# A new order, annealed offline, for the matmuls, evictions and elementwise steps of an attention and snake-MLP kernel

## The chip, the cores and the metric

The kernel runs on one core of one Trainium2 chip. The metric is the device time of an execution in microseconds (us). A core has five engines that each run their own list of instructions in order: TensorE (PE: matmuls and transposes), VectorE (DVE), ScalarE (ACT), GpSimd (POOL), and SyncE (SP), which here only issues DMAs. They wait for each other through semaphores. DMAs are issued by SP, POOL and ACT and run on sixteen DMA engines. Matmul results land in PSUM, which has eight banks of 128 partitions x 512 f32.

## The reference

Inputs are `x` [8, 8, 512, 64] (batch, head, token, dim), `state` [8, 8, 32, 64], `w_in` [512, 2048], `w_out` [2048, 512], `alpha` [2048]; all f32.

```python
scores = scale * x @ state.T; a = softmax(scores);   xread = a @ state      # [8, 8, 512, 64]
scores2 = scale * state @ x.T; a2 = softmax(scores2); sread = a2 @ x         # [8, 8, 32, 64]
y = concatenate([xread, sread], axis=2), heads moved into columns            # [8 * 544, 512]
h = y @ w_in
g = h + sin(alpha * h)**2 / (alpha + 1e-9)
out = g @ w_out                                                              # [4352, 512] f32
```

## The kernel before

All matmuls are bf16 with f32 accumulation. The 4352 rows are worked in nine tiles: tiles t = 0 to 7 hold the 512 `xread` rows of a batch, tile 8 the 256 `sread` rows of all batches. `xread @ w_in` is never built in two steps: for each batch b the kernel makes M = state @ w_in (step `m`, 64x512 pieces on quarters of the array, L488), evacuates it (`me`, L496), and then h = A @ M, where A is the normalised softmax.

The program is a list of steps in a string, `ORDER`. Each word is a method of `Steps` and its arguments; running the list in order appends instructions to the engines' lists, and nothing reorders them later (`tc.manual_schedule()`). So the list fixes the order on each engine; in time, an instruction starts when its engine is free and its semaphores are there. The last letter of many steps picks the engine: A is ACT, V is DVE, G is POOL. The steps that matter here:

- `li.s`, `lo.s`, `lx.b`: loads of a quarter of `w_in` (L282), of `w_out` (L294), of a batch of `x` (L275), all issued by POOL with a cast to bf16.
- `warm_up.n.cols.bank` (L303): n matmuls on zeros, whose result nobody reads.
- `pk.b`, `td.b`: `x` repacked on DVE and transposed by a DMA issued by SP (L389); `sc`, `ex`, `rs`, `rr`, `nm`: scores on PE, exp on ACT, row sums, reciprocal, and the multiply (L201) that makes A; `ad.b`: A transposed by a DMA from SP (L440). Batches 0 and 1 use PE transposes for some of this (`xtq`, `xt`, `at`, copied by `xc`, `ac`).
- `w`, `cs`, `rc`, `xs`: the `sread` side; eight times, once for each batch, feeding tile 8.
- `h.t.f.bank` (L537; L543 for tile 8): the 128-column piece f (0 to 15) of h for tile t, two matmuls of 512 columns (four of 256 for tile 8), into a PSUM bank. `hg` (L552) does one of the two.
- `si.t.f` (L560): sin on ACT, reading the bank. `sq.t.f.E` (L201 on DVE or POOL, L569 on ACT): its square. `gt.t.f` (L576): on DVE, gT = square / alpha + h, reading the bank again. Only after `gt` is the bank free.
- `o.t.st.f0.f1[.bank]` (L587): for row block st (four in a tile, two in tile 8), matmuls of gT piece f by `w_out`, f from f0 to f1, accumulating sixteen in one bank. `oc.t.st.E` (L595) evacuates the bank to an o_sb buffer, `os.t.st` stores it from SP (L602, for tile 8 L605). The last block, 7.3, is cut in columns into 384 and 128 (`oh`, `och`, `osh`).

A PSUM bank holds one thing at a time: a step that names a bank waits for the last reader of what was there. The s and squared-s tiles share ten buffers, gT has 38, o_sb has six.

Of the kernel before, what the change touches and what calls it, by code (L numbers as in the profile page):

```python
# [33 lines left out]
me.1.1.1.A warm_up.2.128.2 gt.0.2 si.0.0 warm_up.2.128.2 warm_up.2.128.6 warm_up.2.128.3
warm_up.2.128.2 warm_up.2.128.6 me.0.1.0.A gt.0.1 sq.0.0.G m.0.2.3.2 si.0.3 m.1.2.5.6 hg.0.4.0.7
me.0.2.0.V me.0.2.1.A hg.0.4.1 sq.0.3.G hg.0.6.0.4 me.1.2.1.V hg.0.6.1 si.0.4 hg.0.7.0.3 hg.0.11.0.2
me.1.2.0.V si.0.6 hg.0.7.1 sq.0.4.G hg.0.5.0.6 gt.0.0 hg.0.5.1 si.0.7 hg.0.11.1 hg.0.8.0.5 hg.0.8.1
sq.0.6.A gt.0.3 sq.0.7.G o.0.3.0.2.0 si.0.5 gt.0.4 o.0.3.2.3 o.0.0.0.2.1 si.0.11 o.0.0.2.3 gt.0.6
sq.0.5.G o.0.0.3.4 o.0.2.0.1.7 si.0.8 o.0.3.3.5 sq.0.11.A gt.0.7 hg.0.9.0.4 sq.0.8.G o.0.2.1.2
gt.0.5 o.0.2.2.4 hg.0.9.1 gt.0.11 o.0.0.4.5 hg.0.10.0.3 si.0.9 o.0.2.4.5 gt.0.8 o.0.0.5.6 o.0.3.5.6  # L40
sq.0.9.A o.0.3.6.8 pk.1.0.V hg.0.10.1 xt.1.1.6 pk.1.1.V si.0.10 gt.0.9 xt.1.0.2 xc.1.1.0.A sq.0.10.G
o.0.2.5.6 xc.1.1.1.V xc.1.0.0.A o.0.0.6.7 xc.1.0.1.V o.0.0.7.8 o.0.2.6.7 sc.1.1.5 gt.0.10 sc.1.0.4
m.0.3.6.2 ex.1.0 o.0.2.7.8 me.0.3.0.V o.0.1.0.3.3 me.0.3.1.V o.0.1.3.6 hg.0.13.0.6 o.0.1.6.7 ex.1.1
rs.1.0 hg.0.13.1 m.1.3.2.4 si.0.13 o.0.1.7.8 rr.1.0 rs.1.1 nm.1.0.0.4.G o.0.1.8.9 hg.0.12.0.5
o.0.3.8.9 rr.1.1 hg.0.12.1 me.1.3.0.V o.0.0.8.9 nm.1.1.0.4.G o.0.1.9.10 o.0.0.9.10 me.1.3.1.V
si.0.12 o.0.0.10.11 o.0.3.9.11 sq.0.13.G ad.1 hg.0.15.0.2 sq.0.12.A o.0.1.10.12 hg.0.15.1 gt.0.12
o.0.2.8.10 si.0.15 o.0.2.10.11 gt.0.13 o.0.0.11.12 hg.0.14.0.4 sq.0.15.A hg.0.14.1 o.0.3.11.13
si.0.14 gt.0.15 o.0.0.12.13 o.0.1.12.13 o.0.3.13.14 sq.0.14.A pk.2.0.V o.0.1.13.14 pk.2.1.V h.1.2.5
gt.0.14 h.1.4.6 td.2 si.1.2 lx.3.0.1 h.1.0.2 si.1.4 o.0.0.13.15 sq.1.2.V h.1.1.4 si.1.0 gt.1.2
sq.1.4.G o.0.3.14.16 si.1.1 o.0.2.11.13 sq.1.0.A oc.0.3.V h.1.6.5 sq.1.1.G gt.1.4 o.0.2.13.14 os.0.3  # L50
h.1.3.0 si.1.6 gt.1.0 o.0.1.14.16 si.1.3 sq.1.6.G h.1.13.6 gt.1.1 oc.0.1.A o.0.2.14.15 o.0.0.15.16
si.1.13 h.1.15.2 sq.1.3.G lx.4.0.1 gt.1.6 os.0.1 o.0.2.15.16 oc.0.0.A h.1.5.4 sq.1.13.V oc.0.2.V
si.1.15 h.1.7.3 os.0.0 gt.1.3 o.1.1.0.1.5 si.1.5 os.0.2 h.1.8.1 sq.1.15.G gt.1.13 o.1.1.1.2 si.1.7
o.1.2.0.2.7 sq.1.5.A o.1.1.2.3 sq.1.7.G h.1.12.0 gt.1.15 si.1.8 h.1.9.6 gt.1.5 o.1.2.2.3 si.1.12
sq.1.8.G o.1.2.3.5 gt.1.7 si.1.9 o.1.1.3.4 h.1.10.2 sq.1.12.A pk.3.1.V h.1.11.4 sq.1.9.G gt.1.8
o.1.2.5.6 si.1.10 o.1.2.6.7 gt.1.12 h.1.14.3 si.1.11 sq.1.10.G o.1.2.7.8 gt.1.9 sc.2.1.1 si.1.14
o.1.1.4.7 sq.1.11.A pk.3.0.V sq.1.14.G o.1.1.7.8 gt.1.10 td.3 o.1.2.8.9 sc.2.0.0 o.1.1.8.9 gt.1.11
# [24 lines left out]
o.2.2.14.15 h.3.4.4 si.3.10 gt.3.15 o.2.1.6.7 sq.3.7.G o.2.1.7.8 si.3.4 o.2.2.15.16 o.2.1.8.10
sq.3.10.A gt.3.9 o.2.1.10.11 sq.3.4.G gt.3.7 o.2.1.11.13 oc.2.2.A o.2.1.13.14 gt.3.10 o.2.1.14.16
os.2.2 h.3.3.0 gt.3.4 oc.2.1.A h.3.12.2 si.3.3 pk.5.1.V o.3.2.0.1.7 os.2.1 m.4.2.1.3.5.6 pk.5.0.V
si.3.12 sq.3.3.V td.5 o.3.3.0.1.4 me.4.2.1.V me.4.2.0.A o.3.2.1.2 sq.3.12.G o.3.3.1.2 me.4.3.0.A
o.3.2.2.3 gt.3.3 o.3.3.2.3 h.3.11.1 me.4.3.1.A gt.3.12 h.4.10.3 si.3.11 h.4.9.5 si.4.10 h.4.12.0
sq.3.11.V h.4.11.6 si.4.9 gt.3.11 sq.4.10.G o.3.2.3.5 si.4.12 o.3.2.5.7 sq.4.9.A o.3.2.7.8 gt.4.10
sq.4.12.G o.3.2.8.10 si.4.11 o.3.2.10.11 gt.4.9 o.3.3.3.5 sq.4.11.A o.3.3.5.6 gt.4.12 o.3.3.6.8
m.4.0.2.1.3.5 gt.4.11 o.3.3.8.9 me.4.1.1.V me.4.0.1.A h.3.13.0 me.4.0.0.A h.4.8.6 me.4.1.0.V
h.4.15.1 si.3.13 h.4.2.5 si.4.8 sq.3.13.V h.4.1.2 lx.6.0.1 si.4.2 gt.3.13 o.3.2.11.12 o.3.1.0.2.3  # L90
si.4.15 o.3.1.2.3 sq.4.8.V o.3.1.3.4 sq.4.2.G si.4.1 gt.4.8 o.3.3.9.12 sq.4.15.A h.4.3.0 sq.4.1.G
gt.4.2 o.3.3.12.13 h.4.13.6 si.4.3 gt.4.15 o.3.3.13.15 si.4.13 sq.4.3.G o.3.3.15.16 gt.4.1 h.4.6.5
# [65 lines left out]
class Steps:  # L158
# [449 lines left out]
    def oh(k, t, st, half, bank):  # L608
        k.o(t, st, 0, k.FT, bank, half=half)
# [54 lines left out]
```

## Time and profile before

| what | us |
|---|---|
| median of 3 runs | 221.41 (221.36 to 221.83) |
| the profiled execution's own time | 221.22 |
| its span | 219.2 |
| PE busy in the span | 211.4 |
| DVE, ACT, POOL busy | 162.9, 173.4, 106.2 |
| landings of `w_in` quarters 0, 1, 2 | 11.83, 14.91, 17.37 |

A span is the time from the first to the last instruction of the program; the time of a run also holds what lies around it. In the groups of the profile, a line reads: source line, engine, operation, output<-inputs, shape, count | busy time, mean ns of one | idle time of that engine just ahead of them and what ended it. In a table by stage, each stretch has its length, then busy time and count of PE, weight loads (PEld), DVE, ACT, POOL, then the granted PE clock, the share of the DMA engines in use, and GB/s. A PE that the profile calls busy may hold overlapping matmuls, so counts and start times are better guides than busy time.

### The profile page before, as it was taken

The page shows a single profiled execution, that of the slowest core. Times are in us where ns is not written, and L with a number is a line of the kernel's source. Part 1 is how long each engine was busy: PE and PEld are TensorE (multiplying, and loading weights), DVE is VectorE, ACT ScalarE, POOL GpSimd, SP SyncE. Part 2 cuts the span into 40 slices and gives each one's busy share as a digit, 9 for nine tenths or more (in the row PEclk, how much of TensorE's full clock was granted, in tenths as well). Part 3 has the DMA queues.
Part 4 walks back from the last instruction along what each step waited for, and adds up shares of the span by engine and source line. Part 5 has one row for each costly group of instructions (what it writes and reads, how often), then busy time and mean ns, then how long its engine had stood idle before and what let it go on. Part 6 is the DMA issues. An engine that isn't in the chain of part 4 may idle for free.

```text
span 219.2 us, 4303 instructions
## 1 busy us (share of the span) xinstructions
PE 211.4 (96%) x1593; PEld 104.5 (48%) x1619; DVE 162.9 (74%) x287; ACT 173.4 (79%) x297; POOL 106.2 (48%) x114
## 2 busy tenths in 40 slices
PE   7989999999999999999999999999999999999994
PEld 3744544444444534444454444454445555665452
DVE  3769996999787789989888788888667987661201
ACT  4799778997998979898996999798848896785111
POOL 5959533895195647753943387273501082121000
PEclk9999999999999999999999999999999999999999
DMA  6999999987491029167145327470220211012042
GB/s 195 178 206 204 205 204 146 217 169 133 101 238 48 3 92 143 57 144 96 48 79 131 109 71 96 134 110 0 48 100 0 98 48 48 0 51 96 1 143 96
DMA packets 38052, 23.48 MB, mean 107 GB/s; under 512 B 20992, under 2 KB 33680, under 8 KB 38032
## 3 DMA queue, kind: packets, MB, share of 16 engines
q1 hardware_dynamic: 26128, 15.08, 26.5%
q0 software_dynamic: 11648, 8.13, 26.0%
q8 instruction: 12, 0.20, 0.3%
q14 instruction: 8, 0.07, 0.1%
q10 hardware_dynamic: 256, 0.01, 0.1%
HBM read 17.44 MB, written 8.91 MB: 120 GB/s over the span
## 4 chain that ended last, share of the span: by engine, by line
PE 90%; DMA 6%; POOL 1%; issue 1%; ACT 0%
PE o_ps L587 54%; PE h_ps L537 22%; DMA w_in_sb<-in_moe_w_in_dram 5%; PE m_ps L488 4%; PE h_ps L543 3%; PE h_ps L552 2%; PE w_ps L450 2%; PE s_ps L399 2%; PE w_ps L461 1%; DMA s<-in_state_dram 1%; POOL w_in_sb L282 1%; PE x_ps L376 0%; POOL st_nat L267 0%; POOL s01b L255 0%; ACT o_sb L595 0%
## 5 line engine op out<-in xcount | busy, mean ns | idle before, releaser
L587 PE MATMUL o_ps<-w_out_sb,gT 128*128 128x512 bf16 (+2 forms) x542 | 133.9, 373 | 1.6 <-issue 1.0
L576 DVE SCALAR_TENSOR_TENSOR gT<-s,inva_sb,h_ps 128x512 bf16<-128x512 bf16 (+1 forms) x144 | 96.8, 713 | 20.4 <-POOL s L201 10.8
L201 POOL TENSOR_TENSOR s<-s 128x512 bf16<-128x512 bf16 (+1 forms) x75 | 75.9, 1022 | 64.4 <-ACT s L560 62.7
L560 ACT ACTIVATE s<-h_ps,alpha_sb 128x512 bf16<-128x512 f32 (+1 forms) x144 | 88.8, 670 | 11.1 <-PE h_ps L543 4.5
L587 PEld LDWEIGHTS <-gT 128*128 128x128 bf16 x560 | 52.3, 98 | 60.3 <-issue 5.0
L537 PE MATMUL h_ps<-AT,M 128*128 128x512 bf16 x219 | 60.0, 379 | 0.3
L537 PEld LDWEIGHTS <-M 128*128 128x128 bf16 x224 | 21.7, 98 | 25.9 <-issue 0.4
L569 ACT ACTIVATE s<-s 128x512 bf16<-128x512 bf16 (+1 forms) x53 | 31.4, 594 | 0.8
L201 POOL TENSOR_TENSOR A<-E,rR 128x512 bf16<-128x512 bf16 x16 | 16.6, 1056 | 23.8 <-ACT o_sb L595 12.9
L595 ACT COPY o_sb<-o_ps 128x512 f32<-128x512 f32 (+2 forms) x24 | 13.7, 570 | 16.6 <-PE o_ps L587 16.5
L496 ACT CAST M<-m_ps 128x512 bf16<-128x512 f32 x35 | 18.6, 594 | 8.2 <-PE m_ps L488 8.2
L496 DVE CAST M<-m_ps 128x512 bf16<-128x512 f32 x29 | 18.9, 679 | 2.5 <-PE m_ps L488 2.1
L595 DVE COPY o_sb<-o_ps 128x512 f32<-128x512 f32 x11 | 7.5, 685 | 12.9 <-PE o_ps L587 12.9
L201 DVE TENSOR_TENSOR s<-s 128x512 bf16<-128x512 bf16 (+1 forms) x16 | 7.0, 439 | 6.2 <-ACT s L560 6.1
L410 DVE TENSOR_REDUCE R<-E 128x16 f32<-128x512 bf16 x16 | 10.4, 657 | 0.7 <-ACT E L406 0.6
L488 PE MATMUL m_ps<-w_in_sb,stT 64*32 64x512 bf16 x256 | 10.2, 382 | 0.1
L468 DVE RECIPROCAL rC<-w_ps 128x128 f32<-128x128 f32 x8 | 7.6, 948 | 3.3 <-PE w_ps L461 3.2
L303 PE MATMUL warm_ps<-warm 128*128 128x128 bf16 (+3 forms) x66 | 8.6, 271 | 1.4 <-DVE warm L209 1.2
L552 PE MATMUL h_ps<-AT,M 128*128 128x512 bf16 x29 | 8.4, 379 | 0.9 <-ACT M L496 0.7
L406 ACT ACTIVATE E<-s_ps 128x512 bf16<-128x512 f32 x16 | 8.8, 602 | 0.4 <-PE s_ps L399 0.4
L543 PE MATMUL h_ps<-xs_all,w_in_sb 128*128 128x256 bf16 x64 | 9.1, 273 | 0.0
L543 PEld LDWEIGHTS <-w_in_sb 128*128 128x128 bf16 x64 | 6.3, 98 | 3.4
(56 smaller groups left out, 101.8 us busy)
## 6 DMA issues: line engine op xcount, KB each, us to landing
out_dram<-o_sb SPq DMA_DIRECT2D x33, 256.0 KB, 2.3
xnat<-in_x_dram POOLq DMA_DIRECT2D x7, 512.0 KB, 7.5
w_in_sb<-in_moe_w_in_dram POOLq DMA_DIRECT2D x4, 512.0 KB, 10.9
w_out_sb<-in_moe_w_out_dram POOLq DMA_DIRECT2D x4, 512.0 KB, 18.0
x<-in_x_dram SPq DMA_DIRECT2D x4, 256.0 KB, 4.2
st_nat<-in_state_dram POOLq DMA_DIRECT2D x1, 256.0 KB, 5.3
out_dram<-o_sb SPq DMA_DIRECT2D x1, 192.0 KB, 1.9
s<-in_state_dram SPq DMA_DIRECT2D x1, 128.0 KB, 2.2
```

Source lines behind the costliest of these rows:

```text
L201: {"V": k.nc.vector, "G": k.nc.gpsimd}[eng].tensor_tensor(out, a, b, ALU.mult)
L410: k.nc.vector.reduce_sum(R[:, g], k.t["E", b][:, g].rearrange("p c (h j) -> p (c h) j", j=k.Ns), axis=AX.X)
L488: k.nc.tensor.matmul(k.t["m", b, s + n, g][o0:o0 + k.Ns, :], k.stT[k.half(r), b * k.G + g, c0:c0 + k.Ns], k.w_in_sb[k.half(r), 2 * g + h, ...
L496: k.copy(eng)(k.t["M", b][:, g, s * k.FW:(s + 1) * k.FW], k.t["m", b, s, g][:])
L537: k.nc.tensor.matmul(hp[:, :n], k.t["M", t][:, g, fs], k.t["AT", t][:, g, :], start=(g == 0), stop=(g == k.G - 1),)
L543: k.nc.tensor.matmul(hp[:, :n], k.w_in_sb[:, q, fs], k.xs_all[:, q].rearrange("p b j -> p (b j)"), start=(q == 0), stop=(q == k.Q - 1),)
L552: k.nc.tensor.matmul(k.t["h", t, f][:], k.t["M", t][:, g, f * k.P:(f + 1) * k.P], k.t["AT", t][:, g, :], start=(g == 0), stop=(g == k.G - 1),)
L560: k.nc.scalar.activation(s[:, :n], k.t["h", t, f][:, :n], ACT.Sin, scale=k.alpha_sb[:, f:f + 1])
L569: k.nc.scalar.activation(s2[:, :n], s[:, :n], ACT.Square)
L576: k.nc.vector.scalar_tensor_tensor(gT[:, :n], k.t["s2", t, f][:, :n], k.inva_sb[:, f:f + 1], k.t["h", t, f][:, :n], ALU.mult, ALU.add,)
L587: k.nc.tensor.matmul(k.t["o", t, st, half][:, cols], k.t["gT", t, f][:, rows], k.w_out_sb[:, f, cols], start=(f == 0), stop=(f == k.FT - 1),)
L595: k.copy(eng)(o_sb[:, cols], k.t["o", t, st, half][:, cols])
```

## The change

The string `ORDER` is replaced as a whole. Three method changes let the new order be finer: opening a bank is a step of its own (`ho`, `oo`), `hg` and `o` issue one matmul, and the first and last matmul of an accumulation are those that come first and last in the list, so that the pieces f of an o block can be added in any order. The computation is the same; there are the same 560 o, 256 + 64 h and 256 m matmuls and the same loads, transposes and stores. Counts that differ: warm-up matmuls 66 to 14; squares on ACT 53 to 32, on DVE 16 to 55, on POOL 75 to 57; five of the sixteen `nm` move from POOL to DVE; the four casts of `x` for batch 0 (`xq`) move from ACT to DVE; M evacuations on ACT 35 to 39, on DVE 29 to 25; o evacuations on DVE 11 to 9. POOL issues its loads in the same order, SP its transposes too, with the stores at other places between them. On SP the last stores were os.6.0, 7.1, 8.1, 8.0, 7.0, 7.3 (384 columns), 7.2, 7.3 (128 columns) and become os.7.3 (384 columns), 6.3, 7.2, 7.1, 7.0, 8.1, 8.0, 7.3 (128 columns).

```diff
 ORDER = """
...
-ac.0.0.V m.0.0.6.4 m.1.0.1.2 lo.3 at.0.1.7 me.0.0.0.V me.0.0.1.A warm_up.2.128.0 warm_up.2.128.3
-me.1.0.1.A ac.0.1.V hg.0.2.0.5 me.1.0.0.V hg.0.1.0.4 hg.0.2.1 hg.0.1.1 hg.0.0.0.0 lx.2.0.1 si.0.2
-hg.0.0.1 m.1.1.6.3 si.0.1 m.0.1.7.2 hg.0.3.0.1 me.0.1.1.A sq.0.2.V hg.0.3.1 sq.0.1.G me.1.1.0.V
-me.1.1.1.A warm_up.2.128.2 gt.0.2 si.0.0 warm_up.2.128.2 warm_up.2.128.6 warm_up.2.128.3
-warm_up.2.128.2 warm_up.2.128.6 me.0.1.0.A gt.0.1 sq.0.0.G m.0.2.3.2 si.0.3 m.1.2.5.6 hg.0.4.0.7
-me.0.2.0.V me.0.2.1.A hg.0.4.1 sq.0.3.G hg.0.6.0.4 me.1.2.1.V hg.0.6.1 si.0.4 hg.0.7.0.3 hg.0.11.0.2
...
-o.8.1.1.2 oc.7.1.A o.8.1.2.3 o.8.0.0.1.6 o.8.1.3.4 os.7.1 o.8.1.4.5 h.8.14.3 o.8.1.5.7 si.8.14
-o.8.0.1.3 sq.8.14.A o.8.0.3.5 gt.8.14 o.8.0.5.7 o.8.1.7.11 o.8.0.7.15 o.8.1.11.16 o.8.0.15.16
-o.7.0.8.9 oc.8.1.A o.7.0.9.10 oc.8.0.V o.7.0.10.12 os.8.1 o.7.0.12.13 os.8.0 o.7.0.13.16 o.7.2.0.2.2
-oc.7.0.A o.7.2.2.5 os.7.0 o.7.2.5.11 oh.7.3.0.1 o.7.2.11.13 och.7.3.0.A o.7.2.13.15 osh.7.3.0
-o.7.2.15.16 oh.7.3.1.4 oc.7.2.V os.7.2 och.7.3.1.A osh.7.3.1
...
+me.0.0.1.A ac.0.1.V m.1.0.3.1 me.1.0.1.A me.1.0.0.V hg.0.0.0 li.2 hg.0.0.1 si.0.0 st_c.0.1.V
+sq.0.0.V ho.0.3.7 hg.0.3.1 lo.0 hg.0.2.0 hg.0.2.1 si.0.2 ho.0.1.3 hg.0.1.1 lo.1 m.0.1.1.6 me.0.1.0.A
+lx.1.0.1 me.0.1.1.V hg.0.1.0 si.0.1 m.1.1.0.5 me.1.1.0.A hg.0.3.0 ho.0.5.1 li.3 hg.0.5.0 hg.0.5.1
+ho.0.4.6 hg.0.4.0 lo.2 lo.3 lx.2.0.1 me.1.1.1.V ho.0.7.5 hg.0.4.1 hg.0.7.1 hg.0.7.0 gt.0.0 si.0.3
+sq.0.2.G gt.0.2 m.0.2.2.0 me.0.2.1.A sq.0.1.G gt.0.1 sq.0.3.G gt.0.3 me.0.2.0.A m.1.2.4.0 me.1.2.1.A
+ho.0.9.3 hg.0.9.1 hg.0.9.0 ho.0.11.2 hg.0.11.0 me.1.2.0.V si.0.4 sq.0.4.V gt.0.4 hg.0.11.1 ho.0.6.0
+hg.0.6.0 oo.0.1.7 si.0.5 sq.0.5.G si.0.7 sq.0.7.V hg.0.6.1 si.0.6 o.0.1.3 o.0.1.1 gt.0.7 si.0.9
+sq.0.9.V oo.0.0.4 o.0.0.1 o.0.0.3 o.0.0.0 o.0.0.2 o.0.1.0 oo.0.2.6 o.0.2.2 sq.0.6.A o.0.2.0 o.0.1.2
+o.0.2.3 gt.0.6 o.0.2.1 gt.0.9 o.0.2.4 oo.0.3.5 o.0.3.3 o.0.3.4 o.0.1.7 o.0.0.4 gt.0.5 ho.0.8.0
...
+o.0.2.5 ex.1.0 rs.1.0 sc.1.1.3 o.0.3.1 me.0.3.1.A ex.1.1 o.0.3.0 rs.1.1 ho.0.12.2 hg.0.12.0 rr.1.0
+pk.1.0.V hg.0.12.1 si.0.12 m.1.3.0.1 me.1.3.0.V me.1.3.1.A ho.0.14.3 hg.0.14.1 hg.0.14.0 o.0.0.8
...
+sq.0.15.V o.0.1.13 gt.0.15 o.0.3.13 o.0.1.15 o.0.2.15 o.0.3.15 h.1.4.1 si.1.4 h.1.6.0 si.1.6
+sq.1.6.G pk.2.0.V o.0.1.9 pk.2.1.V h.1.3.3 si.1.3 oc.0.2.V sq.1.4.V gt.1.4 sq.1.3.V gt.1.3 o.0.1.10
+h.1.7.6 si.1.7 o.0.0.13 sq.1.7.G o.0.3.11 oc.0.3.A gt.1.6 gt.1.7 h.1.13.2 si.1.13 o.0.0.15 h.1.9.1
+si.1.9 h.1.12.5 si.1.12 h.1.15.3 sq.1.9.V gt.1.9 oc.0.1.A oo.1.3.0 o.1.3.3 o.1.3.4 o.1.3.6 oc.0.0.A
+h.1.0.6 si.1.0 sq.1.13.G o.1.3.7 h.1.5.7 oo.1.2.4 o.1.2.9 o.1.2.3 o.1.2.4 o.1.2.6 gt.1.13 si.1.5
...
+osh.7.3.0 o.8.1.5 os.6.3 o.8.0.3 o.7.2.8 oc.7.2.A os.7.2 gt.8.14 o.8.1.14 o.8.0.14 o.7.0.6 o.8.1.13
+o.7.1.14 o.8.1.9 o.8.0.9 o.8.1.12 oc.7.1.A os.7.1 o.8.1.0 o.8.1.8 o.8.1.2 o.7.0.2 oc.7.0.V o.8.0.0
+os.7.0 oc.8.1.A os.8.1 o.8.0.13 o.8.0.11 oc.8.0.V os.8.0 oh.7.3.1.6 och.7.3.1.A osh.7.3.1
 """.split()
...
-        k.t = {}
+        k.t, k.made = {}, {}
...
-    def hg(k, t, f, g, *bank):
-        if g == 0:
-            k.t["h", t, f] = k.ps(bank[0], [k.P, k.S], FP32, "h_ps")
+    def ho(k, t, f, bank):
+        k.t["h", t, f] = k.ps(bank, [k.P, k.S], FP32, "h_ps")
+        k.made["h", t, f] = 0
+
+    def hg(k, t, f, g):
+        k.made["h", t, f] += 1
         k.nc.tensor.matmul(
             k.t["h", t, f][:], k.t["M", t][:, g, f * k.P:(f + 1) * k.P], k.t["AT", t][:, g, :],
-            start=(g == 0), stop=(g == k.G - 1),
+            start=k.made["h", t, f] == 1, stop=k.made["h", t, f] == k.G,
         )
...
-    def o(k, t, st, f0, f1, *bank, half=None):
+    def oo(k, t, st, bank, half=None):
+        k.t["o", t, st, half] = k.ps(bank, [k.P, k.DOUT], FP32, "o_ps")
+        k.made["o", t, st, half] = 0
+
+    def o(k, t, st, f, half=None):
         cols = k.cols(half)
-        if f0 == 0:
-            k.t["o", t, st, half] = k.ps(bank[0], [k.P, k.DOUT], FP32, "o_ps")
         rows = slice(st * k.P, (st + 1) * k.P) if t < k.B else slice(st, k.B * k.Ns, 2)
-        for f in range(f0, f1):
-            k.nc.tensor.matmul(
-                k.t["o", t, st, half][:, cols], k.t["gT", t, f][:, rows],
-                k.w_out_sb[:, f, cols], start=(f == 0), stop=(f == k.FT - 1),
-            )
+        k.made["o", t, st, half] += 1
+        k.nc.tensor.matmul(
+            k.t["o", t, st, half][:, cols], k.t["gT", t, f][:, rows], k.w_out_sb[:, f, cols],
+            start=k.made["o", t, st, half] == 1, stop=k.made["o", t, st, half] == k.FT,
+        )
...
     def oh(k, t, st, half, bank):
-        k.o(t, st, 0, k.FT, bank, half=half)
+        k.oo(t, st, bank, half=half)
+        for f in range(k.FT):
+            k.o(t, st, f, half=half)
```

## The prediction

> **What bounds the kernel now.** I read the page's totals first, then stages, then the timeline at both ends.
>
> ```profile
> span 219.2 us, 4303 instructions
> PE 211.4 (96%) x1593; PEld 104.5 (48%) x1619; DVE 162.9 (74%) x287; ACT 173.4 (79%) x297; POOL 106.2 (48%) x114
> ```
>
> TensorE is busy for 96% of the span. The stage table (busy time of each engine per stretch) says where the rest is.
>
> ```profile
> 0.00:11.85 11.85, 10.19 (x127) 6.63 (x127) 5.98 (x18) 7.45 (x14) 9.52 (x18) 1.00 0.89 187
> 11.85:17.40 5.55, 4.52 (x60) 2.13 (x60) 3.88 (x8) 5.32 (x10) 3.07 (x5) 1.00 1.24 207
> 18.20:28.00 9.80, 9.64 (x83) 4.97 (x84) 9.20 (x17) 8.67 (x16) 6.46 (x7) 1.00 1.30 204
> 28.00:208.00 180.00, 178.31 (x1260) 86.12 (x1282) 142.18 (x245) 149.88 (x256) 86.36 (x86) 1.00 0.45 92
> 216.15:219.20 3.05, 0.00 (x0) 0.00 (x0) 0.00 (x0) 0.27 (x1) 0.00 (x0) 1.00 0.31 107
> ```
>
> See the second column: after 18.2 us PE never idles for long. A dense 512-column matmul takes 0.216 us (ten in 2.16 in the chain of waits). The remaining idle is a slot of 0.216 here and there where a matmul record is missing: every record from 18.2 to 216 starts one issue time after its predecessor. So PE's end is the start of m.0.2 plus the PE work left there. Priced from dense stretches (h or o 0.216, m 0.216, sc 0.233, w 0.466, changes of tile shape 0.09 to 0.13 each way), that work is 198.6; 17.41+198.6=216.0, and the last evacuation does start at 216.15.
>
> ```profile
> 17.41 0.14 PEld L488 LDWEIGHTS <-stT 64*32 64x32 bf16 x16 [0.26 <-DMA w_in_sb<-in_moe_w_in_dram]
> 18.20 2.54 PE L552 MATMUL h_ps<-AT,M 128*128 128x512 bf16 x11 [0.16 <-issue]
> ...
> 207.87 1.49 SPq L605 DMA_DIRECT2D out_dram<-o_sb  x2
> ...
> 216.15 0.27 ACT L595 COPY o_sb<-o_ps 128x128 f32<-128x128 f32 x1 [1.50 <-PE o_ps L587]
> ```
>
> m.0.2 waits for the third w_in load (landed 17.37), which no reordering of compute brings forward. The two stores at L605 are those of tile 8, and they matter below. The profiled execution took 221.22 (span 219.2 plus 2.02 outside), 0.19 under the median; my sum is made against 221.22.
>
> **The change part by part.**
>
> *Loads, transposes, table loads: nothing.* Their order is kept on every queue, apart from stores moved between them on SP; ACT still loads its table as often. Loads run back to back, one landing per 2.54 us, so issuing lo.3 before nm instead of after lands nothing sooner. Every transpose has 3.4 us or more of PE work between its place and its use (3.2 before), except td.7, which stands beside sc.7.0 but may issue some 9 us earlier, when pk.7 is done. If that cover went, the price is a landing, 3 to 5 us. Stores free o_sb 4 us or more ahead of need.
>
> *PE work: -1.3.* Ahead of m.0.2 the new order has 14 hg matmuls where the old had 8: 6 x 0.216 = 1.30. From m.0.2 on there is one more block of m (+0.22) and one block of cs fewer (-0.2). Left at m.0.2: 197.3 instead of 198.6. The 52 dropped warm-up matmuls stood in waits for loads and are worth nothing by themselves.
>
> *New waits in the head: +2.0.* Other durations by form: si 0.695 (three in a row 1.90, so 0.633 in a queue), gt 0.742 (0.68 queued), sq 0.64 on ACT, 0.449 on DVE, 1.05 on POOL, me 0.594/0.679 (ACT/DVE); 0.2 from a matmul's issue end to its reader. (a) m.0.2 needs bank 2 (h.0.0) from gt.0.0, which on DVE stands behind st_c.0.1, sq.0.0 and both me of s=1; DVE then ends gt.0.0 at about 17.5: +0.15. (b) m.1.2 puts its second half into bank 0, which m.0.2 has just filled, and must wait for me.0.2.1 on ACT: 17.56+0.34+0.15+0.55 gives 18.66, where 17.87 is dense: +0.8. (c) Behind it on ACT stand me.0.2.0, me.1.2.1, si 4, 5, 7, 6, 9 and sq.0.6.A: 2x0.55+5x0.633+0.6 ends at 23.55; with sq.0.9.V, gt.0.6 on DVE this frees bank 0 for hg.0.8.0 at 24.37 instead of 23.97: +0.4. (d) me.1.3.0 waits on DVE behind rs, rs, rr, pk (0.66+0.66+0.25+0.43), then gt.0.12 behind it: +0.65. What is queued behind each is PE itself, in order; nothing overtakes. The old order had its evacuations of s=2 in four banks, and none of these waits shows.
>
> *New waits later: +2.3.* The old order gives the median gT 8.2 us between its chain's end and its first o; the new one 5.3, with more h and o tiles open in the eight banks. I summed queued work between a matmul's result and the PE step that needs the buffer. Early in batch 1: from si.1.4, seven si and two oc on ACT (7x0.64+2x0.58+0.2=5.9) must end before h.1.5, 5.4 us of PE work later, and a third oc before o.1.2.9: +0.7; then h.1.1 behind gt.1.14: +0.3. The same sums overrun by 0.2 to 0.5 at batch 2 (ten DVE items from sq.2.4), at batch 4's end and where batches 5 and 6 mix (fifteen DVE items from me.6.3.1). Bounds: 0.8 if only the single-queue overruns count, 4.6 if those that cross engines (s has ten buffers, and si.6.11 now waits on sq.6.4) double my hand sum. On the old order the same sums overrun nowhere (closest 0.09 to spare), as its trace shows. DVE takes 39 more sq, five nm and the x copies (163 to about 180 busy of 219): no bound by itself. nm and the x copy on DVE aren't in the trace: between 0.425 (copy) and 1.056 (nm on POOL); I take 0.45, nearest to the bf16 multiply on DVE; hidden before the w_in landing at 11.83, where the next work waits.
>
> *The tail: +2.8.* In the old order tile 8's stores issue at 207.87 and 208.76, almost eight microseconds before the last. They cost more than others: issue 0.775 and 0.609 against 0.33, and the trace's completion writes end at 211.71 and 212.89: 3.8 and 4.1 after issue, where a 256 KB store of another tile lands in 2.0. Their completions come from 8 engines each instead of 16, and the DMA rate starts low:
>
> ```profile
> 209.00:209.50 0.50, 0.50 (x4) 0.26 (x3) 0.00 (x0) 0.29 (x1) 0.00 (x0) 1.00 0.39 66
> 209.50:210.00 0.50, 0.50 (x4) 0.23 (x3) 0.00 (x0) 0.29 (x1) 0.00 (x0) 1.00 0.45 33
> 210.00:210.50 0.50, 0.50 (x4) 0.20 (x2) 0.00 (x0) 0.00 (x0) 0.00 (x0) 1.00 0.34 49
> ```
>
> Now they are second and third from last. With P as PE's end: last o of tile 8.0 ends at P-0.90 (16x0.056), its evacuation on DVE waits for oc.7.0 and ends at P; SP has os.7.0 from P-0.6, os.8.1 P-0.3, os.8.0 P+0.5, the last store P+1.1. os.8.0 then lands at P+0.5+4.1+0.35 (write to landing, as for os.7.0) = P+4.95; the old last landing was 218.28, P+2.15. +2.8. Bounds: +1.9 if the slow start is missing (32 packets of 0.084 on an engine), +3.3 if the last store queues behind.
>
> Against the change speaks a rule of the Trainium skill, DMA: Bandwidth & Descriptors, "HWDGE ordering" and "How many engines (k)": a copy is spread over the largest k up to 16 that divides both sides' slowest dimension, 8 for a pattern of 8x16 rows. This agrees with the 8 completions; by its 2.0 us fixed part and half the engines, an estimate, one such store would land in 3.2 and the tail would grow by some 2 instead of 2.8.
>
> The clock: the trace's first 512-column matmuls take 0.427 each, and from 5.1 us on 0.216 or less; it shows no return to the slow rate, so by the rows fewer warm-ups cost nothing. The Trainium skill, TensorE: Matmul & The Clock Gate, "The HAM clock gate", would have the clock halve after an idle window of about 3.4 us; were the new head idle for so long, an estimate from it is 3.4 us at half rate, 1.7 us of PE work, part of it hidden by the loads. I count no idle above 1 us there and add nothing.
>
> Sum: 221.22-1.3+2.0+2.3+2.8 = 227.0.
>
> **The rivals.**
> *The waits don't come.* For: most overruns are tenths, and pipelined instructions hide a little. Against: (b) is a wait by the bank numbers alone. 221.2-1.3+0.2+2.8=222.9.
> *The stores are no slower at the end.* For: one pair in the trace, perhaps slowed by os.7.0. Against: its first 36 packets, ahead of os.7.0's, were the slow ones. 221.2-1.3+4.3+0.4=224.6.
> *Waits feed each other.* Ten s buffers and DVE near full: an si that waits holds ACT, which holds a bank. Body waits of 6 to 8: 231 to 233.
> *Faster.* One mechanism: work pulled ahead of the third w_in landing stays ahead, and waits and tail together cost less than the 1.3 gained. With both at 0.2: 220.1. Decides below 1.3; my smallest sum is 1.2 (head) +0.8+1.9 = 3.9.
> The change may also fail to do what it says if transposes move; then batches 5 to 7 wait 3 us, about 229.
>
> **How the numbers follow.** Main case 0.55, waits absent 0.14, stores quick 0.12, feeding each other 0.12, transposes 0.04, faster 0.03. All but the last are slower by over 0.2% (0.44 us, about what a measurement of this kernel can tell from no change): slower 0.96, same 0.01, faster 0.03. Low: -1.3+1.2+0.8+1.9 gives 223.8, opened to 222.6 to take in the case without waits; high: -1.3+2.6+4.6+3.3 gives 230.4.
>
> **What would show it.** After: a PE wait on ACT M between 18.0 and 18.7 and the h.0.8 matmul near 24.4; PE's last matmul near 219; idle of PE before h and o after 18 us of 3 to 5 us in total, released by DVE gT and ACT; L605 issues among the last three and 5 to 6 us from PE's end to the span's end. Wrong if PE is dense after 18 us, if L605 lands in 2 us, or if PE's clock halves in the head.

## The result: slower by 5.6%, more than the forecast

The changed kernel takes 233.96 us (median of 5 runs, 233.60 to 234.66) against 221.41 (5 runs, 221.12 to 221.83): a ratio of 1.0564, with a 95% interval from 1.0543 to 1.0585. The forecast was 227.0 with a range to 230.4. The direction was right; the loss is 12.5 us where 5.8 was forecast.

The page of the changed kernel, the same two lines as were shown of before (busy time of each engine, its share of the span, instructions):

```profile
span 231.8 us, 4149 instructions
PE 213.4 (92%) x1541; PEld 101.5 (44%) x1567; DVE 187.8 (81%) x326; ACT 168.3 (73%) x281; POOL 82.9 (36%) x91
```

The profiled execution took 233.60. PE has idled for 18.4 us where it idled for 7.8, and DVE is busy for 187.8 us where the forecast had about 180. The same stretches as before, with the end at PE's last matmul (length, then PE, weight loads, DVE, ACT, POOL, clock, DMA share, GB/s):

```profile
0.00:11.85 11.85, 9.02 (x90) 4.79 (x92) 7.56 (x20) 7.01 (x13) 7.87 (x16) 1.00 0.90 190
11.85:17.40 5.55, 5.05 (x49) 1.94 (x49) 4.68 (x10) 5.18 (x10) 3.18 (x4) 1.00 1.24 206
18.20:28.00 9.80, 8.98 (x80) 4.45 (x79) 9.09 (x15) 8.02 (x14) 2.76 (x3) 1.00 1.30 204
28.00:208.00 180.00, 172.70 (x1213) 80.61 (x1234) 157.78 (x268) 142.10 (x234) 66.12 (x66) 1.00 0.43 89
225.10:231.80 6.70, 0.04 (x1) 0.00 (x0) 0.00 (x0) 0.27 (x1) 0.00 (x0) 0.89 0.43 127
```

Between 28 and 208 us PE now idles for 7.3 us where it idled for 1.7, and it gets through 1213 matmuls where it did 1260. The last stretch is the end: 6.7 us after PE's last matmul, where before had 3.05. DVE is on the path: of the chain of waits (the work that ended last, followed back step by step to what released it), DVE holds 30% of the span, where the old chain held no DVE at all. The chain before, and after:

```profile
PE 90%; DMA 6%; POOL 1%; issue 1%; ACT 0%
```

```profile
PE 57%; DVE 30%; DMA 4%; ACT 3%; issue 1%; POOL 1%; ACTq 0%
```

To see where the time went I took the prediction's own yardstick. For each matmul group, the dense PE work since m.0.2 (at the prices of the prediction, from 17.41 us) gives the time at which it would start if PE never waited; its real start less that is the lateness. In the changed kernel it reads (all of it worked out from start times, so good to about 0.1 us):

| at | us from the start | lateness |
|---|---|---|
| m.1.2 | 18.1 | 0.4 |
| hg.0.9.1 | 19.0 | 1.0 |
| hg.0.14.1 | 32.6 | 3.0 |
| o.0.2.14 | 38.3 | 4.25 |
| h.1.1 | 53.1 | 5.4 |
| m.3.3 | 83.8 | 6.0 |
| h.4.6 | 119.5 | 9.0 |
| h.7.1, the last step up | 191.8 | 10.2 |

So the account of the profiled execution is 221.22 (before) - 1.3 (PE work ahead of m.0.2) + 10.2 (waits) + 3.6 (end) = 233.7, against 233.60. The prediction had waits of 4.3 and an end of 2.8. The end is mis-sized by 0.8; the waits are mis-sized by 5.9, and that is the question for the experiments.

One row of the groups points to a cause. These are the squares and `x` copies on DVE before the change, then after it (busy, mean ns of one, idle before):

```profile
L201 DVE TENSOR_TENSOR s<-s 128x512 bf16<-128x512 bf16 x15 | 6.7, 449 | 6.2 <-ACT s L560 6.1
L348 DVE COPY xp<-xnat 128x1024 bf16<-128x1024 bf16 x14 | 5.5, 429 | 0.1
```

```profile
L202 DVE TENSOR_TENSOR s<-s 128x512 bf16<-128x512 bf16 x48 | 28.4, 591 | 4.0 <-ACT s L564 3.7
L349 DVE COPY xp<-xnat 128x1024 bf16<-128x1024 bf16 x14 | 7.4, 533 | 0.0
```

The means go from 449 to 591 and from 429 to 533 ns. Sorted in the trace of the changed kernel by what POOL does meanwhile, the 512-column squares take 421 ns where no POOL product runs (24 of 48) and 811 where one runs for most of their time (21), up to 1347. `gt`, which reads `h` from PSUM, takes 744 and 742. The place of one of the steps in lateness shows what that does (timeline: start, length, then engine, line, operation, and idle before with its releaser):

```profile
103.24 1.04 POOL L202 TENSOR_TENSOR s<-s 128x512 bf16<-128x512 bf16 x1 [1.93 <-ACT s L564]
103.28 1.28 DVE L202 TENSOR_TENSOR s<-s 128x512 bf16<-128x512 bf16 x1
...
104.60 1.41 DVE L580 SCALAR_TENSOR_TENSOR gT<-s,inva_sb,h_ps 128x512 bf16<-128x512 bf16 x2
...
105.40 0.59 PE L538 MATMUL h_ps<-AT,M 128*128 128x512 bf16 x2 [0.56 <-DVE gT L580]
```

A DVE square that starts 0.04 us after a POOL product takes 1.28 us; the `gt` behind it is late, the bank is freed late, and PE waits 0.56 us for it.

### The profile page after: what moved, and what is told of

Same layout as the page of the kernel before. It is cut to its first block, busy times and chain, and to the rows that moved or that the text cites. A ratio compares the mean times of both kernels' runs of the same rounds, so it can differ in the third digit from the quotient of the medians.

```text
span 231.8 us, 4149 instructions
## 1 busy us (share of the span) xinstructions
PE 213.4 (92%) x1541; PEld 101.5 (44%) x1567; DVE 187.8 (81%) x326; ACT 168.3 (73%) x281; POOL 82.9 (36%) x91
## 4 chain that ended last, share of the span: by engine, by line
PE 57%; DVE 30%; DMA 4%; ACT 3%; issue 1%; POOL 1%; ACTq 0%
PE o_ps L593 35%; DVE gT L580 13%; PE h_ps L538 11%; DVE s L202 6%; DMA w_in_sb<-in_moe_w_in_dram 3%; PE m_ps L489 3%; PE h_ps L544 3%; DVE rC L469 2%; DVE M L497 2%; PE h_ps L556 2%; DVE xp L349 2%; PE w_ps L451 1%; DVE xs_all L472 1%; DVE R L411 1%; PE s_ps L400 1%
## 5 line engine op out<-in xcount | busy, mean ns | idle before, releaser
L593 PE MATMUL o_ps<-w_out_sb,gT 128*128 128x512 bf16 (+2 forms) x540 | 137.6, 373 | 3.3 <-DVE gT L580 1.4
L202 POOL TENSOR_TENSOR s<-s 128x512 bf16<-128x512 bf16 (+1 forms) x57 | 57.4, 1014 | 96.2 <-ACT s L564 92.1
L538 PE MATMUL h_ps<-AT,M 128*128 128x512 bf16 x220 | 63.3, 379 | 2.9 <-DVE gT L580 2.3
L202 DVE TENSOR_TENSOR s<-s 128x512 bf16<-128x512 bf16 (+1 forms) x55 | 31.3, 570 | 7.3 <-ACT s L564 6.9
L497 ACT CAST M<-m_ps 128x512 bf16<-128x512 f32 x39 | 21.2, 589 | 7.9 <-PE m_ps L489 7.6
L202 POOL TENSOR_TENSOR A<-E,rR 128x512 bf16<-128x512 bf16 x11 | 11.7, 1061 | 32.6 <-DVE rR L417 13.3
L573 ACT ACTIVATE s<-s 128x512 bf16<-128x512 bf16 (+1 forms) x32 | 19.2, 604 | 0.8
L497 DVE CAST M<-m_ps 128x512 bf16<-128x512 f32 x25 | 16.6, 680 | 3.0 <-PE m_ps L489 2.8
L601 DVE COPY o_sb<-o_ps 128x512 f32<-128x512 f32 x9 | 6.2, 689 | 6.0 <-PE o_ps L593 5.9
L556 PE MATMUL h_ps<-AT,M 128*128 128x512 bf16 x31 | 9.0, 381 | 0.7 <-ACT M L497 0.6
L349 DVE COPY xp<-xnat 128x1024 bf16<-128x1024 bf16 x14 | 7.4, 533 | 0.0
```

The source lines that it names most:

```text
L202: {"V": k.nc.vector, "G": k.nc.gpsimd}[eng].tensor_tensor(out, a, b, ALU.mult)
L497: k.copy(eng)(k.t["M", b][:, g, s * k.FW:(s + 1) * k.FW], k.t["m", b, s, g][:])
L538: k.nc.tensor.matmul(hp[:, :n], k.t["M", t][:, g, fs], k.t["AT", t][:, g, :], start=(g == 0), stop=(g == k.G - 1),)
L556: k.nc.tensor.matmul(k.t["h", t, f][:], k.t["M", t][:, g, f * k.P:(f + 1) * k.P], k.t["AT", t][:, g, :], start=k.made["h", t, f] == 1, sto ...
L573: k.nc.scalar.activation(s2[:, :n], s[:, :n], ACT.Square)
L593: k.nc.tensor.matmul(k.t["o", t, st, half][:, cols], k.t["gT", t, f][:, rows], k.w_out_sb[:, f, cols], start=k.made["o", t, st, half] == 1 ...
```

## The experiments

Two theories. C: DVE's bf16 squares and copies are held up by POOL's products, and with 55 squares on DVE instead of 16 this makes DVE late. O: the new order, with its short chains and bank hand-overs, makes all the waits at the durations that the old profile showed. Later a rival Q was added: the place of each square in the engines' queues.

### The price of a DVE square, alone and beside POOL

The kernel before, with instructions added behind its last matmul (the tiles they need, and one matmul into the PSUM bank `wp`, are left out here):

```diff
...
+    for _ in range(16):
+        nc.vector.tensor_tensor(alone[:], k.warm[:], k.warm[:], ALU.mult)
+    for _ in range(40):
+        nc.gpsimd.tensor_tensor(pooled[:], alone[:], alone[:], ALU.mult)
+    nc.vector.tensor_copy(copied[:], alone[:])
+    for _ in range(16):
+        nc.vector.tensor_tensor(beside[:], k.warm[:], k.warm[:], ALU.mult)
+    for _ in range(12):
+        nc.vector.scalar_tensor_tensor(summed[:], alone[:], k.inva_sb[:, 0:1], wp[:], ALU.mult, ALU.add)
+    for _ in range(12):
+        nc.vector.tensor_copy(copied[:], k.warm[:])
```

> The kernel before, with a block appended behind its last step whose results nobody stores: on DVE 16 squares (128x512 bf16, L201's form) with POOL idle; then, while POOL runs 40 such products, 16 more squares, 12 of gt's form (one input from PSUM) and 12 bf16 copies. Theory C (DVE and POOL get in each other's way): the 16 squares alone take 0.42 us each as the ones without POOL do in the changed kernel's trace, those beside POOL about 0.8, copies beside POOL over 0.6 instead of about 0.2 to 0.4, and gt's form 0.74 in both. Theory O (the slow squares of the changed kernel only stand in it where something else was late): 0.42 in both blocks. The time itself says nothing: it is longer by the appended block.

The timeline of the added part:

```profile
215.77 7.29 DVE L644 TENSOR_TENSOR alone<-warm 128x512 bf16<-128x512 bf16 x16
...
223.14 45.71 POOL L646 TENSOR_TENSOR pooled<-alone 128x512 bf16<-128x512 bf16 x40 [24.31 <-DVE alone L644]
223.30 18.93 DVE L649 TENSOR_TENSOR beside<-warm 128x512 bf16<-128x512 bf16 x16
242.16 9.35 DVE L651 SCALAR_TENSOR_TENSOR summed<-alone,inva_sb,z_ps 128x512 bf16<-128x512 bf16 x12
251.42 13.11 DVE L653 COPY copied<-warm 128x512 bf16<-128x512 bf16 x12
```

Sixteen squares take 7.29 us alone (0.424 for one, 0.456 with the gap between two) and 18.93 beside POOL products (1.15 for one, 1.18 with the gap). The twelve bf16 copies beside POOL take 13.11/12 = 1.09 each with the gap; the single copy ahead of them, which started 0.05 us before POOL's first product, took 0.295. The form of `gt`, with one operand in PSUM, takes 0.747 for one (9.35/12 = 0.78 with the gap), where it takes 0.743 in the kernel. POOL's products follow each other every 45.71/40 = 1.14 us; one takes 1.10 beside the squares and 1.04 beside the copies. So when POOL works without a pause, a DVE square takes as long as a POOL product: not the 0.449 of the prediction. Theory C has its mechanism, larger than it expected; what it costs in the kernel is not shown by this.

### Squares narrowed, on DVE and on POOL

In the changed kernel, the squares of one engine are cut to 64 columns, which `gt` then reads over and over (its edit is left out here). Each of the two kernels was timed once:

```diff
-            k.mul(eng, s2[:, :n], s[:, :n], s[:, :n])
+            c = 64 if eng == "V" else n        # "G" in the second kernel
...
+            k.mul(eng, s2[:, :c], s[:, :c], s[:, :c])
```

> The changed kernel, but each square that DVE makes covers only 64 of its columns, which gt then reads over and over: the rest of these squares is left out, order, banks and waits stay. Theory C (DVE time is what was lost): DVE loses 48 x 0.59 + 7 x 0.43 less about 55 x 0.1, some 26 us of work; PE's waits after the third w_in load shrink from 10.2 us to 3 or less, time about 227. Theory O (short chains and bank hand-overs, whatever DVE's load): most waits stay, PE's waits 7 or more, time above 230.

Measured: 229.75 us, the lateness ends at 6.4 instead of 10.2, DVE busy 176.6. This fits neither number. The narrowed squares were no clean removal: alone they took 188 ns, but with a POOL product beside them for most of their time 569, up to 1030, so even a 64-column square waits for POOL.

> The changed kernel, but each square that POOL makes covers only 64 of its columns (the rest left out), so that POOL is nearly idle; DVE's squares stay whole. Theory C: DVE's squares fall from a mean of 0.59 us to about 0.43, DVE's busy time by 8 us or more, PE's waits from 10.2 to about 5, time about 229. Theory O: DVE's squares stay near 0.59, and only chains through a POOL square (57 of 144) get shorter, by 0.9 each; PE's waits fall by 2 or less, time about 232.

Measured: 228.39 us, lateness 5.06, DVE busy 179.3; DVE's full-width squares now average 457 ns (591 before) and its copies 430 (533). This is what C expected: DVE's own work is unchanged, only POOL's products are short, and 5 us of waits are gone. But `gt` waits for POOL's squares too, and these are shorter as well, so the run alone does not settle it.

### Tile 8's stores last, in the kernel before

Only the two stores of tile 8 are moved to just ahead of the last store:

```diff
-... oc.8.0.V o.7.0.10.12 os.8.1 o.7.0.12.13 os.8.0 o.7.0.13.16 ... oc.7.2.V os.7.2 och.7.3.1.A osh.7.3.1
+... oc.8.0.V o.7.0.10.12 o.7.0.12.13 o.7.0.13.16 ... oc.7.2.V os.7.2 os.8.1 os.8.0 och.7.3.1.A osh.7.3.1
```

> The kernel before, with one thing changed: tile 8's two stores are issued by SP just ahead of the very last store instead of eight us earlier; all compute stays. If those two stores are slow by themselves (8 DMA engines, 3.8 to 4.1 us from issue to landing), the span ends 2.5 to 3.6 us later, as in the changed kernel: time 224 to 225. If they were slow only beside os.7.0's store, they land in about 2 us, and the time is 221.4 to 222.2.

Measured: 225.62 us, ratio 1.0170 (1.0125 to 1.0214) to the kernel before on the same chip. The queue of SP in this kernel, from 214.5 us on:

```profile
214.56 1.63 SPq L602 DMA_DIRECT2D out_dram<-o_sb  x2
216.24 1.45 SPq L605 DMA_DIRECT2D out_dram<-o_sb  x2
217.80 0.51 SPq L602 DMA_DIRECT2D out_dram<-o_sb  x1
```

PE ends at 216.0 as it did, and the span at 223.3 instead of 219.2 (profiled execution 225.38 against 221.22, +4.2). That is above the 224 to 225 expected for slow stores. Nothing but the place of two stores is different, so the stores of tile 8 are slow at the end too, without os.7.0's store just behind them, and cost about 4 us where no work hides them. By their semaphores they land 4.2 and 5.1 us after issue, and the last store, issued 0.73 us behind the second, lands 0.2 us after it, 4.5 us after its own issue.

### The engines of the squares, and the order, each alone

The letters behind `sq` and `nm` are swapped between the two orders: first the new order with the old letters, then the old order with the new letters.

```diff
-sq.0.0.V ... sq.0.2.G ... nm.0.0.0.4.V
+sq.0.0.G ... sq.0.2.V ... nm.0.0.0.4.G
```

> The new order word for word, but every square and every normalising multiply on the engine that the old order gave it (53 squares on ACT, 16 on DVE, 75 on POOL; all nm on POOL). The result is computed in full. Theory C (DVE's squares and copies and POOL's products hold each other up, so DVE is late): the waits of PE fall from about 10 us to 4 to 6, since 16 squares on DVE instead of 55 meet POOL, and the time falls by 4 to 6 us, to 228 to 230; the end, with its 6.6 us after PE, stays. Theory O (the order itself, with its short chains and bank hand-overs, makes the waits at the old prices): the time stays within 1.5 us of the changed kernel's, 232.5 to 235; it may even rise, since ACT, with 21 squares more, has the longer queue.

Measured: 264.53 us, ratio 1.1953 (1.1935 to 1.1971). Both theories missed by 30 us. What DVE waits for in this kernel (total us, times, longest):

```profile
DVE gT L580 <- POOL s L202: 35.2, 35, 4.0
DVE gT L580 <- ACT s L573: 23.5, 17, 2.8
```

In the changed kernel the same two rows are 7.3 (12 times) and 2.5 (4 times). A square that is put on POOL at the place where the order had DVE make it, just ahead of its `gt`, lets DVE wait for the whole POOL product and for those queued ahead of it. The order and the letters are one thing; this run changes the queues so much that it says nothing about C or O.

> The old order word for word, but every square and every normalising multiply on the engine that the new order gave it (32 squares on ACT, 55 on DVE, 57 on POOL; five nm on DVE). The result is computed in full. Theory C: DVE goes from 163 to about 185 us busy and its bf16 squares beside POOL products take 0.8 instead of 0.45; the old order leaves the median gT 8.2 us, so part of this is hidden, but PE waits on DVE appear after 18 us: 2 to 5 us of them, 223.5 to 226.5. Theory O: the old order's slack takes it up, no waits, 221 to 222.

Measured: 228.97 us, ratio 1.0348 (1.0329 to 1.0367), with 8.2 us of lateness at the end of PE's work. The letters alone cost the old order 7.75 us, more than C expected. By the lesson of the run before, part of it may be misplaced squares; the last run of the experiments tells how much.

### The end of the new order

Two rewrites of the new order's last words, with the same steps (the evacuation of 7.2 moves from ACT to DVE). In the first, tile 8 is finished and stored ahead of the last blocks of tile 7:

```diff
-o.8.0.15 oh.7.3.0.5 ... osh.7.3.0 ... os.7.2 ... os.7.1 ... os.7.0 oc.8.1.A os.8.1 ... os.8.0 oh.7.3.1.6 och.7.3.1.A osh.7.3.1
+o.8.0.15 ... os.8.1 ... os.8.0 oh.7.3.0.5 och.7.3.0.A osh.7.3.0 ... os.7.2 ... os.7.1 ... os.7.0 oh.7.3.1.6 och.7.3.1.A osh.7.3.1
```

> The new order up to its last few dozen words; there tile 8 is finished and its two stores are issued ahead of the last blocks of tile 7, as in the old order. The result is computed in full. If the late stores of tile 8 make the longer end (6.6 us after PE's last matmul instead of 3.05): the end shrinks to about 3.1 us and the time falls by 3.0 to 3.6, to 230.4 to 231. If the end is long for another reason: no change, 234.

Measured: 232.68 us, 1.3 less than the changed kernel instead of 3.0 to 3.6. PE ends at the same time. The stores of tile 8 issue at 221.3 and 222.2 instead of 224.8 and 225.7, but now all five stores of tile 7 are issued between 224.0 and 227.1, in the time that PE gives to the last matmuls, and land 3.3 to 4.1 us after issue instead of the usual 2; the end is 5.6 us. The second rewrite spreads them:

```diff
+... o.8.1.14 oc.8.1.A os.8.1 o.8.0.14 oc.8.0.V os.8.0 o.7.1.9 o.7.1.14 oc.7.1.A os.7.1 o.7.0.1 o.7.0.12 o.7.0.6 o.7.0.2
+oc.7.0.V os.7.0 oh.7.3.0.5 och.7.3.0.A osh.7.3.0 o.7.2.7 o.7.2.9 o.7.2.13 o.7.2.8 oc.7.2.V os.7.2 oh.7.3.1.6 och.7.3.1.A
+osh.7.3.1
```

> The new order up to its last 65 words; there tile 8 is finished first and its two stores issue some 6 us ahead of the last store, and the five stores of tile 7 are spread over those 6 us, where the run before had five within 3 us (224.0 to 227.1) and won only 1.3. The result is computed in full. If the two slow stores, and how close behind them the others stand, make the end: 3.0 to 3.8 us from PE's last matmul to the end of the span instead of 6.6, and 230.3 to 231.5. If the end's length has another cause: 232.5 to 234.

Measured: 230.97 us, 3.0 less than the changed kernel, ratio to before 1.0444 (1.0422 to 1.0466). The time is in the range, but the other sign was missed: from PE's last matmul to the end of the span it is 4.2 us in the profiled execution (the slowest of four, 231.56), for the 3.0 to 3.8 expected and 3.1 in the kernel before. Tile 8's stores issue at 220.4 and 221.3, and the five of tile 7 behind them, at 222.0 to 226.2, land 4.9, 5.0, 3.7, 3.2 and 2.7 us after issue. So most of the longer end is a matter of stores: how late the two slow ones are issued, and how close the rest stands behind them.

A fourth kernel had both the old letters in the new order and the first of these tails:

> Both edits at once: the new order with the old engines for squares and nm, and tile 8 finished ahead of the last blocks of tile 7. The result is computed in full. Theory C: both gains add up, 224.5 to 227; what is then left above the kernel before is the new order's own waits, 4 to 6 us, less the 1.3 us of PE work that it moves ahead of the third w_in landing. Theory O: only the end is gained, 230 to 231.5.

It took 263.66 us (ratio 1.1919, 1.1898 to 1.1941), 0.9 less than with the old letters alone, and says no more than the run with those.

### Squares of the same length that POOL does not touch

This run tells C from Q: DVE's squares keep their places and their length alone, POOL's products stay as they are, and only the form changes, to a product of half the columns with an operand in PSUM, which `gt` reads twice.

```diff
-            k.mul(eng, s2[:, :n], s[:, :n], s[:, :n])
+            if eng == "V":
+                c = n // 2
...
+                k.nc.vector.tensor_tensor(s2[:, :c], k.t["h", t, f][:, :c], s[:, :c], ALU.mult)
+            else:
+                k.mul(eng, s2[:, :n], s[:, :n], s[:, :n])
```

> The new order word for word, POOL's products at full size and in their places. Each square that DVE makes (55 of them) is replaced by a product of about the same length when alone, but of another form: 256 columns (128 for tile 8) of h in PSUM by s, an estimated 0.42 to 0.48 us by the rows of gt (0.743 for 512 columns, 0.479 for 256), where the bf16 square takes 0.421 alone and 0.811 beside POOL; gt reads that half twice. The rest of the square is left out, so the output is not the reference's. Theory C (it is the bf16 form beside POOL that makes DVE late): no such product is longer than 0.5, DVE is busy for 180 to 183 instead of 187.8, the waits of PE end at 5 to 6.5 us of lateness instead of 10.2, and the time is 229 to 231. Rival Q (the squares' places in the queues, POOL's included, make the waits, and the narrowed squares of the two earlier runs helped because they were short): the products take the same 0.45, the waits stay at 9 to 10.5, and the time is 233 to 234.5.

Measured: 228.60 us (227.89 to 231.10), ratio 1.0371 (1.0309 to 1.0433), 5.4 us less than the changed kernel. The totals of this kernel's page:

```profile
PE 212.0 (94%) x1541; PEld 101.4 (45%) x1567; DVE 179.5 (79%) x326; ACT 167.7 (74%) x281; POOL 82.7 (37%) x91
```

and the group of the new products:

```profile
L578 DVE TENSOR_TENSOR s<-h_ps,s 128x256 bf16<-128x256 f32 x48 | 20.2, 420 | 4.2 <-ACT s L564 3.7
```

The products take 421 ns with no POOL product running and 420 beside one; DVE's busy time drops to 179.5 us, the "about 180" that the prediction had counted on. At the place that was shown of the changed kernel:

```profile
99.80 1.04 POOL L202 TENSOR_TENSOR s<-s 128x512 bf16<-128x512 bf16 x1 [1.93 <-ACT s L564]
99.84 0.42 DVE L578 TENSOR_TENSOR s<-h_ps,s 128x256 bf16<-128x256 f32 x1
...
100.29 0.75 DVE L587 SCALAR_TENSOR_TENSOR gT<-s,inva_sb,h_ps 128x512 bf16<-128x512 bf16 x1
...
100.80 1.03 PE L538 MATMUL h_ps<-AT,M 128*128 128x512 bf16 x4
```

The DVE product stands 0.04 us behind the POOL product as before, takes 0.42 instead of 1.28 us, and PE's four h matmuls run on with no wait between the second and the third. The lateness ends at 4.6 instead of 10.2: 1.0 at sc.1.0, 1.9 at hg.0.14.1, 3.1 at h.1.1, 3.2 at o.1.1.11, and no step above 0.5 after that. What lateness gains at 84 to 120 us (3.0 in the changed kernel) is 0.5 here. C's three numbers (180 to 183, 5 to 6.5, 229 to 231) each came out a little better than their ranges, and Q's 9 to 10.5 and 233 to 234.5 did not come. Theory C holds and Q falls as the cause of most of the waits. Of the 10.2 - 4.6 = 5.6 us, 0.3 is no contention: in this execution the first `w_in` load landed at 11.80 instead of 12.13 and m.0.2 started 0.32 earlier, 5.37 us behind that landing in both. So the contention of the squares costs 5.3 us. One wait that stays, 0.4 at h.1.8, stands behind an `x` copy on DVE that took 1.30 us beside a POOL product:

```profile
48.04 1.30 DVE L349 COPY xp<-xnat 128x1024 bf16<-128x1024 bf16 x1
...
49.26 2.71 DVE L594 SCALAR_TENSOR_TENSOR gT<-s,inva_sb,h_ps 128x512 bf16<-128x512 bf16 x4
...
50.05 1.25 PE L538 MATMUL h_ps<-AT,M 128*128 128x512 bf16 x4 [0.41 <-DVE gT L594]
```

> The kernel of the run with the old order and the new engines (228.97 us, 8.2 us of lateness on PE), with DVE's 55 squares replaced in the same way: 256 columns of h in PSUM by s, read twice by gt, the rest left out, so the output is not the reference's. DVE's squares there averaged 0.532 (0.414 alone, 0.762 beside POOL), 16 of 48 beside POOL. Theory C alone: the 8.2 us go down by 3 to 5 (16 squares by 0.35 us, and what they delay), to 224 to 226. Rival Q (each engine's list was written for its own letters, and a letter changed in place puts a square behind others on that engine): no more than 1.5 us is gained, 227.5 to 229.

Measured: 225.65 us, ratio 1.0199 (1.0177 to 1.0221), 3.3 us less than with bf16 squares; the lateness ends at 5.1 instead of 8.2. Both are in C's ranges. The 5.1 that stay are there with the squares' contention gone; that they come from squares at places written for another engine is argued from the run with 264.53 us, not shown.

No version here beats the kernel before: the best one that computes the whole result in the new order is the one with the spread stores, at 230.97 us.

## Why the prediction was wrong, point by point

**Where the old kernel was bound, and PE work of -1.3.** Right for the kernel before and for the PE work: m.0.2 starts at 17.49, 0.08 us later than it did, and the account above closes to 0.1 us with it. But in the changed kernel the third `w_in` load, landed at 17.25, is not what it waits for; that is bank 2, freed by gt.0.0, as (a) below shows. The 52 dropped warm-up matmuls cost nothing that shows: from 5.4 us on, matmuls of 128 columns start 0.056 us apart and those of 512 columns 0.216, as in the kernel before. (The granted clock cannot show this: it reads 1.00 in the first 5 us of both kernels too, where the 512-column matmuls are 0.427 apart.)

**Waits in the head, +2.0.** Right in its sum at the old prices, by half of its terms; that the sum agrees is in part luck. (a) and (b) are there:

```profile
16.65 2.06 DVE L580 SCALAR_TENSOR_TENSOR gT<-s,inva_sb,h_ps 128x512 bf16<-128x512 bf16 x3
17.49 0.41 PE L489 MATMUL m_ps<-w_in_sb,stT 64*32 64x512 bf16 x8
17.97 1.71 ACT L497 CAST M<-m_ps 128x512 bf16<-128x512 f32 x3 [0.39 <-PE m_ps L489]
18.10 0.91 PE L489 MATMUL m_ps<-w_in_sb,stT 64*32 64x512 bf16 x8 [0.20 <-DVE gT L580]
18.61 0.10 PEld L489 LDWEIGHTS <-stT 64*32 64x32 bf16 x5 [0.42 <-issue]
```

(a): the first of the three gt, gt.0.0, ends at 17.39 (forecast: about 17.5), and m.0.2 starts 0.1 us behind it, 0.25 behind the landing. (b): the first M evacuation on ACT ends at 18.56, and the second half of m.1.2 starts at 18.61; the prediction writes 18.66, though its terms add up to 18.60. From m.0.2 to hg.0.9.1 lateness grows by 0.9, for the 0.8 forecast; that the first half of m.1.2 waits for a gT too (0.20) was not listed.

(c) nearly fell: lateness grows by 0.13 only between hg.0.9.1 and 25.7 us, and the two h.0.8 matmuls start at 24.07. (d) fell as priced: without the contention o.0.2.12 does not wait for gt.0.12 at all. In their place stand two waits on ACT that were not listed: 0.46 at sc.1.0 for an xT copy, and 0.64 at hg.0.12.1, whose M evacuation stands on ACT behind the first exp of batch 1 and its table load (1.28 us):

```profile
PE h_ps L556 <- ACT M L497: 0.6, 1, 0.6
```

With the squares out of POOL's way the head ends at 1.9, for 2.0 forecast; in the changed kernel it is at 3.0 by hg.0.14.1 and at 4.25 by o.0.2.14, with waits at m.0.3 (0.73), o.0.2.12 (0.80) and o.0.2.14 (0.49), which are 0.13 and nothing without the contention.

**Waits later, +2.3.** The failed step. With the squares out of POOL's way they are 4.6 - 1.9 = 2.7, near the 2.3 of the hand sums, but the places agree only in part: the 0.23 at h.1.1, for 0.3, was forecast; the 0.4 at h.1.8 behind the stretched copy and the 0.3 at h.7.1, for an xs product on DVE, were not. In the kernel as it is, the waits come to 10.2 in all, 6.0 of them behind o.0.2.14, above the upper bound of 4.6, and the prediction's sentence that fell is the one on DVE: squares at 0.449, "163 to about 180 busy of 219: no bound by itself". The 0.449 was the mean of 15 squares of which 11 met no POOL product and two more met one for under half of their time. The new order puts 48 of that size on DVE, 21 of them mostly beside POOL, and these took 0.811. DVE was busy 8 us longer than counted (187.8 for about 180), at the very places where a `gt` stands behind a square and a bank behind the `gt`.

The profile of before held the sign of it: two of the 15 squares ran mostly beside POOL and averaged 618 ns, with 414 to 658 as the range of all. I read a mean of 449 and took it as one price. The Trainium skill says it outright, SBUF — State Buffer, "Who interferes with whom": a DVE instruction with two SBUF inputs contends with a GpSimd instruction that reads SBUF, and one with at most one SBUF input outside the two-port modes does not. The runs agree with both halves: 0.424 to 1.15 for the bf16 square, 0.42 and 0.42 for the product with an operand in PSUM, 0.744 and 0.742 for `gt`. The diff moved 39 squares to DVE; with some 20 of them at 0.81 instead of 0.42, DVE comes to 180 + 8 = 188 us, which is what was measured.

**The nm and `x` copies on DVE at 0.45.** Too low, and small: the five nm take 0.809 on average (0.691 alone, 1.276 beside POOL), in the upper part of the bounds; the four casts of `x` 0.487.

**The end, +2.8.** The mechanism held and the size was off: +3.6, above the upper bound of 3.3. Tile 8's stores issue at 224.78 and 225.67, 0.53 us behind PE's end for the second, as forecast (0.5). By its semaphore this second store lands at 230.71, 5.0 us after its issue, where the prediction had 4.1 + 0.35 = 4.45; in the kernel before it was 4.8, so the landing was read too early. The last store lands at 230.90, 0.2 us behind it and 4.5 us after its own issue, where the old last store took 1.8. These two, 0.6 and 0.2, are the 0.8 us above the forecast. The kernel before with only these two stores moved lost 4.2.

**The rivals.** "Waits feed each other", at 231 to 233 and with a chance of 0.12, came nearest in time, and its body waits of 6 to 8 fit the 6.0 measured behind o.0.2.14. It had DVE near full, but its mechanism, s buffers and ACT's queue, is not the one that the runs show; whether the ten s buffers add to the lateness no run tells. The rivals without waits and with quick stores fell. That transposes move did not show: no wait of PE above 0.2 us is released by a DMA after the `w_in` loads.

## What to carry to other kernels

Before you take an instruction's price from a mean, ask with what it ran at the same time, and whether the change alters that: for a bf16 square on DVE the price was 0.42 us with POOL still and 0.8 to 1.2 beside a POOL product, and in the kernel before 13 of 15 had stood apart from POOL's products for most of their time. The engine letters of an order and the order itself belong together, so swap them only together, and look for the cause of a wait with an instruction of the same length and another form, rather than by making one short. And look at what the last stores are before you look at the last matmul: two stores with half the DMA engines cost 4 us more at the end than 8 us earlier.

## What the runs showed of the hardware

DVE beside POOL is not a matter of taking turns for whole instructions. Alone, a DVE square takes 0.424 us, and a POOL product takes 1.04 beside instructions of DVE that read PSUM; one after the other would make 1.46 for a pair. With both engines running without a pause a pair takes 1.18 (18.93/16): one square goes with each product. So DVE pays nearly all of it: its square is stretched to 1.15, about POOL's length, and POOL's product grows by 6%, to 1.10. The section of the Trainium skill named above has one engine block the other for a whole instruction; the recorded times show less than that, and whether a part of each lies outside the block no run here tells. A narrow square does not escape: 64 columns take 0.188 alone and 0.569 beside POOL, one of them 1.03, as if it waited for what is left of the POOL product.

A store of tile 7 is slow when it stands close behind the two of tile 8, whose completions come from 8 engines each: 4.4 us from issue to landing in the kernel before (issued 1.1 us behind), 4.5 in the changed kernel, 3.3 to 4.1 and 2.7 to 5.0 in the two rewrites of the end, where one by itself takes 1.8 to 2.0. Closeness alone does much less: three stores within 1.0 us in the changed kernel, issued from 220.7 us on with none of tile 8 ahead, took 1.9, 2.2 and 2.4.
